# Batch 2's q^T on TensorE, batch 3's loads earlier, k loaded with q and v from batch 4 on

## The chip, the cores and the metric

The kernel runs on one core of a Trainium2 chip. The metric is the device time of one execution in microseconds (us); the figure for the kernel before is the median of three runs. A profiled execution gives the rest: which engine worked when, what each instruction waited for, and when the transfers landed.

The core has a matrix engine (TensorE, PE in the profile; PEld is its weight load), a vector engine (VectorE, DVE), an activation engine (ScalarE, ACT), a general engine (GpSimd, POOL) and a synchronising engine (SyncE, SP). In this kernel GpSimd issues the loads from main memory, which turn float32 into float16 on the way, and SyncE issues, in one queue that keeps its order, the stores of the output and the DMA transposes.

## The reference

Attention with k and v projected along the sequence (1024 rows to 64), for 8 batches of 8 heads with head size 64, followed by a gated layer over the 512 features of all heads:

```python
k_proj = np.einsum('ks,bhsd->bhkd', E, k)
v_proj = np.einsum('ks,bhsd->bhkd', F, v)
scores = np.matmul(q, k_proj.transpose(0, 1, 3, 2)) / sqrt(64)
attn = softmax(scores)                       # over the 64 projected rows
attn_out = np.matmul(attn, v_proj)           # 8 x 8 x 1024 x 64
x = attn_out.transpose(0, 2, 1, 3).reshape(8192, 512)
g = np.maximum(x @ w1, x @ w2)               # 8192 x 1024
out = g @ w_out                              # 8192 x 512, float32
```

The kernel computes the gated layer in another form (the maximum as a ReLU of x @ (w1 - w2) plus x @ w2, and products of 2 x 2 blocks with seven products instead of eight), which the change does not touch. The scores need q with the head size on the partitions, q^T (`qt`), and the projected k in the same way (`kpt`). How these two transposes are made, and when q, k and v are loaded for them, is what the change is about.

## The kernel before

The program sets the order of every engine's instructions itself. Buffers that matter here:

```python
kvq = ctx.enter_context(tc.tile_pool(name="kvq", bufs=4))     # k, v and q of all batches, in turn
...
def att_banks(dtype=FP32):                                    # two PSUM tiles of two banks, in turn
    return ps.tile(
        [128, 2, 512 if dtype == FP32 else 1024], dtype, tag="att", bufs=2, name="att_ps"
    )
```

A load takes the oldest of the four kvq tiles, and waits until that tile has been read for the last time: k and v by the projections, q by its transposes. The projections (L180) of a batch, and the two ways to transpose:

```python
def step_kv(t, h0=0, h1=H, which="kv", att=False, dma=False):
    kv_ps = att_banks()[:, 0, :] if att else mm_bank()
    ...                                          # products with E and F, L180; copies by ACT (k) and DVE (v, L195)
            if dma:
                nc.vector.tensor_copy(out=kp[:, :, 1, :], in_=kp[:, :, 0, :])     # L197
                step_kpt_dma(t)                  # kpt by DMA transpose, L222

def step_kpt(t, h0=0, h1=H, att=False):          # kpt by TensorE, L210, and a copy by DVE, L215

def step_gate(t):                                # GpSimd reads kpt: what it issues after comes later
    nc.gpsimd.tensor_copy(out=junk, in_=t["kpt"][0:1, 0, 0:1])

def step_qt(t, h0, nh=2, i0=0, i1=NI):           # q^T of nh heads by TensorE
    qt_ps = mm_bank(FP16)
    ni = i1 - i0
    for h in range(nh):
        for i in range(ni):
            nc.tensor.transpose(                 # L236
                out=qt_ps[:, (h * ni + i) * 128 : (h * ni + i + 1) * 128],
                in_=t["q"][:, h0 + h, 2 * (i0 + i) : 2 * (i0 + i) + 2, :],
                identity=ident16,
            )
    nc.vector.tensor_copy(                       # L241
        out=t["qt"][:, h0 : h0 + nh, i0 * 128 : i1 * 128],
        in_=qt_ps[:, 0 : nh * ni * 128].rearrange("q (h n) -> q h n", h=nh),
    )

def step_qt_dma(t, h0=0, h1=H):                  # q^T by DMA transpose, in the queue of SyncE
    nc.sync.dma_start_transpose(                 # L248
        out=t["qt"][:, h0:h1].rearrange("q h (i p) -> q (h i) p", p=128),
        in_=t["q"][:, h0:h1].rearrange("p h c d -> p (h c d)"),
    )
```

Attention goes in four parts per batch, of two heads each. `step_sc` makes scores in an attention tile (L260) and their exponential; `step_da` makes the sums (dn) and the values (at) in two attention tiles (L365), the logarithm of the sums (L374), its negative exponential (L377, a slot later), and the product on DVE (L381, a slot after that). From batch 3 on, `step_group` makes the scores in other banks (L280).

The rest of TensorE's work is the gated layer: 16 units (two per batch, n from 0), each with seven up products (L621) and seven down products (L699). The down products of unit n alternate with the up products of unit n + 1, in two halves h. The program names the slots between them: ("G", n, h) opens a half, ("U", n, h, i) is the i-th up product of it, and steps are hung behind slots:

```python
def loads(b, *names):
    for n in names:
        b_ = b + (n == "k")
        if b_ < B:
            load_all(tiles[b_], b_, n, {"k": k, "v": v, "q": q}[n])
...
t = tiles[2]
at_slot(("P", 0, 6, 0), new_attn, t)
at_slot(("P", 0, 6, 0), step_qt_dma, t, 0, H // 2)
at_slot(("P", 0, 6, 0), step_qt_dma, t, H // 2, H)
at_slot(("G", 1, 0), step_kv, t, 0, H, "kv", True)
at_slot(("G", 1, 0), loads, 3, "v", "q", "k")
at_slot(("U", 1, 0, 1), step_kpt, t, 0, H, True)
for key, s_, p in (
    (("U", 1, 0, 6), step_sc, 0), (("U", 1, 1, 0), step_da, 0), (("U", 1, 1, 2), step_sc, 1),
    (("U", 1, 1, 5), step_da, 1), (("G", 2, 0), step_sc, 2), (("U", 2, 0, 2), step_da, 2),
    (("U", 2, 0, 4), step_sc, 3),
):
    at_slot(key, s_, t, p)

for b in range(3, B):
    t = tiles[b]
    n = 2 * b - 4
    at_slot(("G", n, 0), new_attn, t)
    at_slot(("G", n, 0), step_qt_dma, t, 0, H // 2)
    at_slot(("G", n, 0), step_qt_dma, t, H // 2, H)
    at_slot(("U", n, 0, 1), step_kv, t, 0, H, "kv", True, b > 3)
    if b > 3:
        at_slot(("U", n, 0, 6), step_gate, t)
    else:
        at_slot(("U", n, 0, 3), step_kpt, t, 0, H, True)
    at_slot(("U", n, 0, 6), loads, b + 1, "v", "q", "k")
```

So in the kernel before, the loads behind a batch are v and q of the next batch and k of the one after it; q^T comes by DMA from batch 2 on, and kpt by DMA from batch 4 on.

Of the kernel before, what the change touches and what calls it, by code (L numbers as in the profile page):

```python
# [9 lines left out]
FP16 = mybir.dt.float16  # L10
# [6 lines left out]
def kernel(  # L17
# [12 lines left out]
    nc = tc.nc  # L30

    B, H, S, D = q.shape
# [4 lines left out]
    NI = NC // 2  # L37
# [22 lines left out]
    def mm_bank(dtype=FP32, n=None):  # L60
        if n is None:
            n = turn.pop(0)
            turn.append(n)
        return ps.tile([128, 512 if dtype == FP32 else 1024], dtype, tag=f"mm{n}", name="mm_ps")

    def att_banks(dtype=FP32):
        return ps.tile(
            [128, 2, 512 if dtype == FP32 else 1024], dtype, tag="att", bufs=2, name="att_ps"
        )
# [27 lines left out]
    def load_all(t, b, n, src):  # L97
        alloc(t, n)
        load(t, n, src, b, 0, H)
# [23 lines left out]
    for f0 in range(0, DF, 256):  # L123
        for w_sb, w in ((w2_sb, moe_w2), (w1_sb, moe_w1)):
            nc.gpsimd.dma_start(
                out=w_sb[:, :, f0 : f0 + 256],
                in_=w[:, f0 : f0 + 256].rearrange("(r p) f -> p r f", p=128),
# [5 lines left out]
    junk = const.tile([1, 1], FP16)  # L133
# [16 lines left out]
    for i in range(2):  # L150
        eft_ps = mm_bank()
        for c in range(NC):
            nc.tensor.transpose(
                out=eft_ps[:, c * KP : (c + 1) * KP],
                in_=ef_v[:, i, c, :],
# [68 lines left out]
        )  # L224


    def step_gate(t):
        nc.gpsimd.tensor_copy(out=junk, in_=t["kpt"][0:1, 0, 0:1])


    def step_qt(t, h0, nh=2, i0=0, i1=NI):
        qt_ps = mm_bank(FP16)
        ni = i1 - i0
        for h in range(nh):
            for i in range(ni):
# [9 lines that stand above are left out]
# [274 lines left out]
    U = {(b, o): {"n": n, "b": b, "o": o, "t": tiles[b]} for n, (b, o) in enumerate(units)}  # L519
# [260 lines left out]
    t = tiles[0]  # L780
# [4 lines left out]
    step_kpt(t, 0, 4)  # L785
    warm(2)
    step_qt(t, 0, 4, 0, NI // 2)
    step_qt(t, 0, 4, NI // 2, NI)
    warm(2)
    two_sc(t, 0, 0)  # L790
# [7 lines left out]
    two_inv(t, 0, 0)  # L798
    warm(4)
    step_qt(t, 4, 4, 0, NI // 2)  # L800
    step_qt(t, 4, 4, NI // 2, NI)
    warm(2)
# [20 lines left out]

    def loads(b, *names):
        for n in names:
            b_ = b + (n == "k")
            if b_ < B:
                load_all(tiles[b_], b_, n, {"k": k, "v": v, "q": q}[n])

    slots = [  # L830
        (0, u0[0]), (None, f(two_at, 1, 1)), (1, u0[1]), (None, lambda: loads(1, "v", "q", "k")),
        (None, wd[1]), (2, u1[0]), (3, u1[1]), (4, u0[2]), (None, wt[0]), (5, u0[3]),
        (None, wd[2]), (None, wt[1]), (6, u1[2]), (7, u1[3]), (8, u0[4]), (9, u0[5]), (None, wd[3]),
# [30 lines left out]
    def at_slot(key, s, *a):  # L864
        steps.setdefault(key, []).append(lambda: s(*a))
# [11 lines left out]
    t = tiles[1]  # L877
    at_slot((0, 19), new_attn, t)
    at_slot((0, 19), lambda: turn.__setitem__(slice(None), [2, 3]))
    for n, x in enumerate((  # L880
        "kv", "", "kpt", "qt0 qt1", "sc0", "qt2 qt3", "dn0 sc1 in0", "", "dn1 sc2 at0 in1", "",
        "dn2 sc3 at1 in2", "", "dn3 at2 in3", "at3", "",
    )):
        key = ("P", 0, (n - 1) // 2, (n - 1) % 2) if n else (0, 19)
        for name in x.split():
            if name[0] == "k":
                if name == "kpt":
                    at_slot(key, step_kpt, t, 0, H, True)
                else:
                    at_slot(key, step_kv, t)  # L890
                    at_slot(key, loads, 2, "v", "q")
            else:
                i = int(name[2])
                s_ = {"qt": step_qt, "sc": step_sc,
                      "dn": step_dn, "in": step_inv, "at": step_at}[name[:2]]
                at_slot(key, s_, t, 2 * i if name[:2] == "qt" else i)
                if name == "qt3":
                    at_slot(key, loads, 2, "k")
        if n in (1, 5):
            at_slot(key, step_t, 1, (0, 1) if n == 1 else (2, 3))  # L900
        if 6 <= n < 10:
            at_slot(key, sums_x, U[0, 1], ((2, 0, 1, 3)[n - 6],))


    t = tiles[2]
    at_slot(("P", 0, 6, 0), new_attn, t)
    at_slot(("P", 0, 6, 0), step_qt_dma, t, 0, H // 2)
    at_slot(("P", 0, 6, 0), step_qt_dma, t, H // 2, H)
    at_slot(("G", 1, 0), step_kv, t, 0, H, "kv", True)
    at_slot(("G", 1, 0), loads, 3, "v", "q", "k")  # L910
    at_slot(("U", 1, 0, 1), step_kpt, t, 0, H, True)
    for key, s_, p in (
        (("U", 1, 0, 6), step_sc, 0), (("U", 1, 1, 0), step_da, 0), (("U", 1, 1, 2), step_sc, 1),
        (("U", 1, 1, 5), step_da, 1), (("G", 2, 0), step_sc, 2), (("U", 2, 0, 2), step_da, 2),
# [7 lines that stand above are left out]
        at_slot(("G", n, 0), new_attn, t)  # L922
        at_slot(("G", n, 0), step_qt_dma, t, 0, H // 2)
        at_slot(("G", n, 0), step_qt_dma, t, H // 2, H)
        at_slot(("U", n, 0, 1), step_kv, t, 0, H, "kv", True, b > 3)
        if b > 3:
            at_slot(("U", n, 0, 6), step_gate, t)
        else:
            at_slot(("U", n, 0, 3), step_kpt, t, 0, H, True)
        at_slot(("U", n, 0, 6), loads, b + 1, "v", "q", "k")  # L930
    for n in range(2, 2 * B - 1):
        for h in range(2):
            m = 2 * (n - 2) + h
# [2 lines left out]
            b, p = 3 + (m - 1) // 4, (m - 1) % 4  # L936
# [75 lines left out]
```

## Time and profile before

| | us |
| --- | --- |
| time, median of 3 runs (349.24 to 350.76) | 349.68 |
| span of the profiled execution | 348.9 |
| TensorE busy (93% of the span) | 325.7 |
| VectorE busy (69%) | 240.6 |
| ScalarE busy (65%) | 226.2 |
| DMA transposes of q: 12, median from issue to landing | 5.4 |
| loads of k, v, q (1024 KB each in float16), median to landing | 17.9, 10.5, 17.1 |
| chain that ended last: PE 73%, DMA 13%, DVE 6% of the span | |

How to read it: TensorE is the engine that is busy nearly all the time, and the chain of work that ended last runs through it for 73% of the span. The 13% of DMA in that chain are stretches in which the end waited for a transfer. A row of the profile names the line of the kernel, the engine, what the instruction writes and reads, how often, and the time it took; a wait names who waited for whom. A transfer has an issue on its queue (how long the queue was held by it) and a landing.

### The profile page before, as it was taken

The numbers are of one execution on the slowest core, as the hardware profiler recorded it, in microseconds if no ns is written. First come the engines' busy times: TensorE is split into PE (matmuls) and PEld (weight loads), VectorE is DVE, ScalarE is ACT, GpSimd is POOL, SyncE is SP. The second block draws the span as 40 slices with busy tenths as digits, with TensorE's granted clock in tenths as the row PEclk, the third lists the DMA queues.
The fourth block names the chain that finished last, engine by engine and source line by source line (L and its number), as shares of the span: only waits on it lengthen the run. The fifth ranks groups of instructions, "written<-read, shape, count | busy, mean of one in ns | idle before, by whom it ended". The sixth has DMA issues, their size and how long they took to land.

```text
span 348.9 us, 7297 instructions
## 1 busy us (share of the span) xinstructions
PE 325.7 (93%) x3004; PEld 245.2 (70%) x3004; DVE 240.6 (69%) x426; ACT 226.2 (65%) x354; POOL 33.9 (10%) x50
## 2 busy tenths in 40 slices
PE   8969999899891799999999999999999999999994
PEld 4534547577561588788877888688878887888884
DVE  1364898985681186779687868768677968677572
ACT  2585322948671578778876887678778887755541
POOL 8532003020120010030002000020000000000000
PEclk9998999999997699999999999999999999999999
DMA  8999999999999984669987998889290302112032
GB/s 157 205 196 202 207 207 207 214 209 191 215 189 170 181 133 110 153 122 193 238 194 106 172 243 174 151 123 234 66 199 20 104 25 98 60 62 92 31 120 92
DMA packets 75089, 52.90 MB, mean 152 GB/s; under 512 B 28848, under 2 KB 74928, under 8 KB 75056
## 3 DMA queue, kind: packets, MB, share of 16 engines
q0 software_dynamic: 30336, 28.31, 52.1%
q1 hardware_dynamic: 44720, 24.12, 29.9%
q8 instruction: 23, 0.38, 0.4%
q14 instruction: 10, 0.08, 0.1%
HBM read 57.15 MB, written 16.78 MB: 212 GB/s over the span
## 4 chain that ended last, share of the span: by engine, by line
PE 73%; DMA 13%; DVE 6%; ACT 3%; POOL 2%; issue 2%; DVEq 0%; SPq 0%; ACTq 0%; POOLq 0%
PE mm_ps L699 36%; PE mm_ps L621 21%; DMA qt_sb<-q_sb 6%; PE mm_ps L467 4%; DMA v_sb<-in_v_dram 3%; PE att_ps L180 3%; DMA out_dram<-o_sb 3%; PE att_ps L365 2%; PE mm_ps L280 2%; PE mm_ps L503 2%; DMA kpt_sb<-kp_sb 1%; DVE o_sb L723 1%; PE mm_ps L180 1%; POOL q_sb L102 1%; POOL k_sb L102 1%
## 5 line engine op out<-in xcount | busy, mean ns | idle before, releaser
L592 ACT COPY p_sb<-mm_ps 128x512 f32<-128x512 f32 x172 | 97.9, 596 | 37.6 <-PE mm_ps L621 22.4
L699 PEld LDWEIGHTS <-big 128*128 128x128 f16 x768 | 73.8, 99 | 15.6 <-issue 6.6
L636 DVE TENSOR_TENSOR gt_sb<-mm_ps,p_sb 128x512 f16<-128x512 f32 x56 | 38.5, 688 | 62.6 <-PE mm_ps L621 41.4
L699 PE MATMUL mm_ps<-T_sb,big 128*128 128x256 f16 x576 | 78.7, 276 | 0.0
L621 PE MATMUL mm_ps<-big,big 128*128 128x256 f16 x336 | 50.4, 272 | 0.1
L621 PEld LDWEIGHTS <-big 128*128 128x128 f16 x448 | 43.8, 98 | 6.0 <-issue 0.2
L699 PEld LDWEIGHTS <-gt_sb 128*128 128x128 f16 x384 | 35.6, 98 | 13.1 <-issue 8.9
L699 PE MATMUL mm_ps<-wo_sb,gt_sb 128*128 128x256 f16 x256 | 42.7, 273 | 0.5 <-ACT o_sb L767 0.5
L621 PEld LDWEIGHTS <-wd_sb 128*128 128x128 f16 x336 | 33.1, 98 | 4.1
L621 PE MATMUL mm_ps<-xt_sb,wd_sb 128*128 128x256 f16 x224 | 33.9, 274 | 0.0
L299 ACT ACTIVATE ex_sb<-mm_ps 128x512 f16<-128x512 f32 x40 | 21.7, 596 | 17.2 <-PE mm_ps L280 17.2
L381 DVE TENSOR_TENSOR xt_sb<-att_ps,ld_sb 128x1024 f16<-128x1024 f32 x24 | 29.3, 1221 | 3.6 <-ACT ld_sb L377 3.5
L723 DVE TENSOR_TENSOR o_sb<-mm_ps,p_sb 128x512 f32<-128x512 f32 x32 | 21.9, 685 | 8.6 <-PE mm_ps L699 5.1
L377 ACT ACTIVATE ld_sb<-ld_sb 128x1024 f32<-128x1024 f32 x24 | 26.3, 1095 | 0.1
L374 ACT ACTIVATE ld_sb<-att_ps 128x1024 f32<-128x1024 f32 x24 | 24.8, 1033 | 0.6 <-PE att_ps L365 0.6
L699 PE MATMUL mm_ps<-m_sb,xt_sb 128*128 128x256 f16 x128 | 24.4, 273 | 0.0
L671 ACT ACTIVATE gt_sb<-mm_ps 128x512 f16<-128x512 f32 x28 | 16.8, 599 | 8.4 <-PE mm_ps L621 8.4
L582 DVE TENSOR_TENSOR big<-gt_sb 128x1024 f16<-128x1024 f16 x32 | 21.9, 685 | 0.3
L639 DVE TENSOR_SCALAR gt_sb<-gt_sb 128x512 f16<-128x512 f16 (+1 forms) x56 | 20.5, 366 | 1.9
L699 PE MATMUL mm_ps<-wo_sb,big 128*128 128x256 f16 x128 | 21.5, 273 | 0.0
L699 PE MATMUL mm_ps<-T_sb,gt_sb 128*128 128x256 f16 x128 | 21.5, 273 | 0.0
L699 PEld LDWEIGHTS <-xt_sb 128*128 128x128 f16 x192 | 18.8, 98 | 2.2
(104 smaller groups left out, 430.6 us busy)
## 6 DMA issues: line engine op xcount, KB each, us to landing
out_dram<-o_sb SPq DMA_DIRECT2D x63, 256.0 KB, 4.0
k_sb<-in_k_dram POOLq DMA_DIRECT2D x7, 1024.0 KB, 17.9
v_sb<-in_v_dram POOLq DMA_DIRECT2D x7, 1024.0 KB, 10.5
q_sb<-in_q_dram POOLq DMA_DIRECT2D x7, 1024.0 KB, 17.1
big<-in_moe_w_dram POOLq DMA_DIRECT2D x8, 256.0 KB, 13.0
k_sb<-in_k_dram POOLq DMA_DIRECT2D x4, 256.0 KB, 6.8
q_sb<-in_q_dram POOLq DMA_DIRECT2D x4, 256.0 KB, 7.9
v_sb<-in_v_dram POOLq DMA_DIRECT2D x2, 512.0 KB, 12.3
```

Of the source, the lines that this page charges most:

```text
L299: nc.scalar.activation(out=t["ex"][p][:, e, :], in_=banks[e], func=ACTF.Exp, scale=scale)
L374: nc.scalar.activation(out=ld, in_=dn_ps, func=ACTF.Ln)
L377: nc.scalar.activation(out=ld, in_=ld, func=ACTF.Exp, scale=-1.0)
L381: nc.vector.tensor_tensor(out=t["xt"][:, p, :, :], in0=at_ps, in1=ld, op=ALU.mult)
L582: nc.vector.tensor_tensor(out=S(i), in0=x, in1=y, op=op)
L592: copy(out=x, in_=bank)
L621: nc.tensor.matmul(out=bank[:, m * W : (m + 1) * W], lhsT=w_[:, n_, (2 * d + m) * 128 : (2 * d + m + 1) * 128], rhs=a[:, n_, :], start=(n ...
L636: nc.vector.tensor_tensor(out=c_blk(j, c), in0=two(x), in1=two(y), op=ALU.add)
L639: nc.vector.tensor_scalar_max(ap, ap, 0.0)
L671: nc.scalar.activation(out=out, in_=in_, func=ACTF.Relu)
L699: nc.tensor.matmul(out=bank[:, i * CH : (i + 1) * CH], lhsT=a(c)[:, i * 128 : (i + 1) * 128], rhs=w_(c), start=(n is not None and m == (lo ...
L723: nc.vector.tensor_tensor(out=o_sb, in0=two(x), in1=two(y), op=ALU.add)
```

## The change

It does four things. The q^T of batch 2 is made by TensorE, two heads at a time in an attention tile, behind four of the up products, instead of two DMA transposes. The loads of q and v of batch 3 (q now first) are released by the projections of batch 2, as before; k of batch 4 is no longer among them. From batch 4 on the k, v and q of one batch are loaded together, behind the gate, which now also stands behind batch 3's kpt and reads its last head instead of its first. For that, batch 3's kpt comes by DMA transpose, like that of the batches after it. What it is for: DMA transposes of q should not run beside loads, and each set of loads should start only when the transposes of the batch before it are done.

```diff
--- before.py
+++ after.py
@@ -224,12 +224,12 @@
         )
 
 
-    def step_gate(t):
-        nc.gpsimd.tensor_copy(out=junk, in_=t["kpt"][0:1, 0, 0:1])
-
-
-    def step_qt(t, h0, nh=2, i0=0, i1=NI):
-        qt_ps = mm_bank(FP16)
+    def step_gate(t, n="kpt"):
+        nc.gpsimd.tensor_copy(out=junk, in_=t[n][0:1, H - 1, 0:1])
+
+
+    def step_qt(t, h0, nh=2, i0=0, i1=NI, att=False):
+        qt_ps = att_banks(FP16)[:, 0, :] if att else mm_bank(FP16)
         ni = i1 - i0
         for h in range(nh):
             for i in range(ni):
@@ -823,7 +823,7 @@
 
     def loads(b, *names):
         for n in names:
-            b_ = b + (n == "k")
+            b_ = b + (n == "k" and b < 3)
             if b_ < B:
                 load_all(tiles[b_], b_, n, {"k": k, "v": v, "q": q}[n])
 
@@ -904,11 +904,11 @@
 
     t = tiles[2]
     at_slot(("P", 0, 6, 0), new_attn, t)
-    at_slot(("P", 0, 6, 0), step_qt_dma, t, 0, H // 2)
-    at_slot(("P", 0, 6, 0), step_qt_dma, t, H // 2, H)
     at_slot(("G", 1, 0), step_kv, t, 0, H, "kv", True)
-    at_slot(("G", 1, 0), loads, 3, "v", "q", "k")
+    at_slot(("G", 1, 0), loads, 3, "q", "v")
     at_slot(("U", 1, 0, 1), step_kpt, t, 0, H, True)
+    for i, key in enumerate((("U", 1, 0, 0), ("U", 1, 0, 3), ("U", 1, 0, 5), ("U", 1, 1, 1))):
+        at_slot(key, step_qt, t, 2 * i, 2, 0, NI, True)
     for key, s_, p in (
         (("U", 1, 0, 6), step_sc, 0), (("U", 1, 1, 0), step_da, 0), (("U", 1, 1, 2), step_sc, 1),
         (("U", 1, 1, 5), step_da, 1), (("G", 2, 0), step_sc, 2), (("U", 2, 0, 2), step_da, 2),
@@ -922,12 +922,9 @@
         at_slot(("G", n, 0), new_attn, t)
         at_slot(("G", n, 0), step_qt_dma, t, 0, H // 2)
         at_slot(("G", n, 0), step_qt_dma, t, H // 2, H)
-        at_slot(("U", n, 0, 1), step_kv, t, 0, H, "kv", True, b > 3)
-        if b > 3:
-            at_slot(("U", n, 0, 6), step_gate, t)
-        else:
-            at_slot(("U", n, 0, 3), step_kpt, t, 0, H, True)
-        at_slot(("U", n, 0, 6), loads, b + 1, "v", "q", "k")
+        at_slot(("U", n, 0, 1), step_kv, t, 0, H, "kv", True, True)
+        at_slot(("U", n, 0, 6), step_gate, t)
+        at_slot(("U", n, 0, 6), loads, b + 1, "k", "v", "q")
     for n in range(2, 2 * B - 1):
         for h in range(2):
             m = 2 * (n - 2) + h
```

## The prediction, made before the changed kernel ran

> **What bounds the kernel now.** I read the engine totals first (TensorE busy 325.7 of 348.9 us), then the busy tenths by slice:
>
> ```profile
> PE   8969999899891799999999999999999999999994
> PEclk9998999999997699999999999999999999999999
> DMA  8999999999999984669987998889290302112032
> ```
>
> TensorE is full in nearly every slice but the thirteenth (104.7 to 113.4 us, a 1), and there its granted clock falls as well. From 122 to 300 us the list of waits shows only one DMA wait of TensorE itself, 0.3 us. So whatever is to be gained lies before 121 us. The waits from 48 to 122 us, the rows that bear on it:
>
> ```profile
> POOL k_sb L102 <- DMA qt_sb<-q_sb: 16.5, 1, 16.5
> PE mm_ps L280 <- DMA qt_sb<-q_sb: 9.1, 1, 9.1
> ACT o_sb L767 <- DMA out_dram<-o_sb: 2.5, 1, 2.5
> PE att_ps L260 <- DMA qt_sb<-q_sb: 0.8, 1, 0.8
> PE att_ps L365 <- DVE vp_sb L195: 0.7, 1, 0.7
> PE mm_ps L699 <- ACT o_sb L767: 0.5, 1, 0.5
> ```
>
> Nearly all of TensorE's lost time goes back to q^T by DMA transpose. The big wait, in the timeline of TensorE (start, us, engine, line):
>
> ```profile
> 105.97 0.39 PE L365 MATMUL att_ps<-ex_sb,vp_sb 64*64 64x512 f16 x4
> 115.50 0.64 PE L280 MATMUL mm_ps<-qt_sb,kpt_sb 64*64 64x512 f16 x4 [9.14 <-DMA qt_sb<-q_sb]
> 116.08 2.74 PE L699 MATMUL mm_ps<-T_sb,big 128*128 128x256 f16 x12
> 118.61 0.90 PE L621 MATMUL mm_ps<-xt_sb,wd_sb 128*128 128x256 f16 x4
> ```
>
> L280 is the first score product of batch 3. Why its q^T is late is in the timelines of the store and transpose queue, and of the queue of loads:
>
> ```profile
> 69.25 14.66 SPq L248 DMA_TRANSPOSE qt_sb<-q_sb  x2
> 83.95 10.01 SPq L714 DMA_DIRECT2D out_dram<-o_sb  x5
> 94.06 21.23 SPq L248 DMA_TRANSPOSE qt_sb<-q_sb  x2
> 144.00 4.98 SPq L248 DMA_TRANSPOSE qt_sb<-q_sb  x2
> ```
>
> ```profile
> 92.70 0.88 POOL L102 DMA_DIRECT2D k_sb<-in_k_dram  x1 [16.54 <-DMA qt_sb<-q_sb]
> 98.01 0.88 POOL L102 DMA_DIRECT2D v_sb<-in_v_dram  x1 [4.43 <-PE att_ps L180]
> 98.87 0.88 POOL L102 DMA_DIRECT2D q_sb<-in_q_dram  x1
> ```
>
> The same pair of transposes holds the queue 4.98 us in the steady part (144 us) but 21.23 us at 94.06, where k, v and q of batch 4 load beside it. Batch 2's pair (14.66 us) runs beside the loads of k3, v3 and q3, and keeps the stores behind it until 83.95.
>
> **What the Trainium skill says.** "DMA: Bandwidth & Descriptors", section "Queues, rings and completion order": each DMA engine takes turns packet by packet between the queues that have work. The trace agrees in kind: transposes beside three loads land after 21.4 and 19.7 us, alone after 5.0 and 4.7. "TensorE: Matmul & The Clock Gate", Part 4 (PE-mode transpose): a full 128x128 transpose in one go, into PSUM, with a VectorE copy to follow, about 275 ns in one kernel's context. Here it is recorded at 219 ns, but pipelined: 16 of them, L236, run from 58.27 to the next product at 59.16, 56 ns each. The same page, Part 1 (What's actually happening): after an idle window of about 3.4 us the clock halves and comes back after a busy window of the same length. The windows of the trace agree: granted clock 0.70 over 105 to 115 us, 0.50 over 115 to 118, 0.80 over 118 to 121, 1.00 after.
>
> **Removed.** Batch 2's two DMA transposes go, so qt of batch 2 no longer waits for them (0.76 us), stores are not held in the queue, and the ACT copy of the output at 92.97 with the product behind it (0.47 us) comes in time. Batch 3's k projection is transposed by DMA instead of 16 PE transposes (101.11 to 101.48: 0.37 us of TensorE). And the loads of batch 4 now stand behind a gate that reads the end of batch 3's kpt, so batch 3's q^T no longer meets them: 9.14 us of wait, and the slow clock behind it. Its size: L280 started 0.58 us before the next product instead of 0.34 (as four 64x512 products take at 102.67), 12 products took 2.53 us (116.08 to 118.61) instead of 12 x 0.109 = 1.31, four took 0.73 instead of 0.44: 0.24 + 1.22 + 0.29 = 1.75 us. Sum: 0.76 + 0.47 + 0.37 + 9.14 + 1.75 = 12.5 us.
>
> **Do the q^T come in time?** Batch 2's transposes need q2, landed at 53.66 + 15.5 = 69.2; the first is asked for at 75.25, after unit 2's first up product. For batch 3: q3 is issued at 74.4, now ahead of v3, with only the rest of k3 beside it (landing at 59.62 + 16.0 = 75.6). An undisturbed pair of loads lands 9.5 us after the first issue and 17.0 after the second (227.06 and 227.92): q3 at 84, v3 at 92. The order on the queue is eight stores, then the pair of transposes. The eighth store follows unit 1's last down product, before at 93.6; with TensorE 2 us later there (below), 94.9. The pair then holds the queue 5.0 to 6.2 us (the steady pairs), landing at about 102. The projections of batch 3 (before 95.82) need v3, at about 97.8: in time. kpt by DMA: from the start of the projection to its landing the steady batches take 145.79 to 153.0, 7.2 us: 105. The first score product of batch 3 will be asked for at 106.4 + 3.2 (added work, below) - 0.76 - 0.47 - 0.37 = 108.0. Slack 3 us, so I expect no wait.
>
> **Added.** 32 PE transposes at 56 ns: 1.8 us on the engine that bounds. Four VectorE copies of 128x1024 at 0.68 us (the row qt_sb<-mm_ps, median 681 ns): 2.7 us, mostly beside other work, since VectorE was busy 8.4 of 10 us (70 to 80) and 6.4 (80 to 90). But they also delay things that TensorE waits for. (a) The first copy stands ahead of L636 at 77.39, whose end (78.08) releases the product at 78.12: 0.68 of delay against 0.45 of transposes, 0.24 us of new wait. (b) The attention banks are two tiles in turn. Before, the turn in batch 2's stretch was kv A, kpt B, scores A, sums B, values A, scores B; now it is kv A, qt0 B, kpt A, qt1 B, qt2 A, scores0 B, sums A, values B, qt3 A, scores1 B. qt3 thus waits for the logarithm that reads the sums (ends 85.14; 86.7 with the shift of 1.6): 0.2 us. And scores1 takes the tile of the *values*, read last by VectorE's L381 (86.26 to 87.49; shifted 87.83 to 89.06), while scores1 would start at 85.88 + 1.6 + 0.2 + 0.45 = 88.1: about 1.0 us of new wait. Sum of the added: 1.8 + 0.24 + 0.2 + 1.0 = 3.2 us.
>
> **Later batches.** From batch 4 on the three loads k, v, q of one batch follow one gate, instead of v, q and the next k. q is now last of three. The last of three landed at 155.37 + 22.0 = 177.4 and 191.40 + 22.5 = 213.9; the transposes that need q start at 178.82 and 215.24. That leaves 1.3 to 1.4 us, and another 1 to 2 us before kpt's transpose behind them is held up. I expect it to fit and cost nothing. For batch 4 the loads go out at about 105 and land by 129; its transposes come at 144 - 9 = 135.
>
> **Sum.** 12.5 removed, 3.2 added, net 9.3 us: 349.7 - 9.3 = 340.4. From 121 us on TensorE was gapless, so a shift there passes to the end unchanged. I put 340.3.
>
> **Rivals.** *Collision moves instead of going:* v3 is still landing when the transposes of q3 run, or a store holds them up, and the first scores of batch 3 still wait 2 to 5 us, with a dip of the clock: 343 to 346. For it: one in-order queue, and kpt3 added to it. Against: v3 should have landed 3 us before, and 3 us of slack. *q last of three arrives late:* each of batches 5 to 7 waits 1 to 2 us, 3 to 5 us in all: 344. For it: only 1.3 us of slack at the transpose, and all three loads of batch 7 now go where only two went. Against: the k load that was last landed before the transposes each time. *The attention banks cost more:* VectorE, nearly full there, lets every copy through to TensorE, 4 x 0.68 instead of 1.4: 341.7. *The removed waits were all, with the new bank waits hidden:* 349.7 - 12.5 + 1.8 = 339.0.
>
> **Range and chances.** The gain of 9.14 is one recorded wait with a cause that the change takes away twice (no batch 4 loads beside it, no transposes of batch 2 ahead), so most cases end between 339 and 342.5. The first two rivals give the upper end. 2% is 7.0 us, at 342.7. Range 338.3 to 343.3; faster by over 2% 0.82, within 2% 0.15, slower 0.03 (it would take late loads in every later batch).
>
> **What would show it.** Slice 13 at 9 for TensorE and its clock; no wait of L280 on qt_sb; the transposes of batch 3 starting near 95 and holding the queue 5 to 6 us; k4 issued near 105; L236 by 32 more, new rows of qt_sb<-att_ps near 0.68 us; a wait of about 1 us of L260 on VectorE's L381 near 88 us. I am wrong if the L280 wait stays above 2 us, if L280 of batches 5 to 7 waits for DMA, or if the 75 to 95 us stretch grows by more than 4 us.

## The result and the profile after

| | before | changed |
| --- | --- | --- |
| time, median of 4 runs each | 349.46 us (347.29 to 350.76) | 338.41 us (338.06 to 339.83) |
| ratio, with its 95% interval | | 0.970 (0.964 to 0.975) |
| span of the profiled execution | 348.9 us | 336.3 us |
| batch 2's projections to batch 3's first scores (first L180 of batch 2 to first L280) | 43.86 us (71.64 to 115.50) | 35.17 us (69.85 to 105.02) |
| from there to the end | 233.40 us | 231.28 us |

The changed kernel is 11.05 us faster; 9.3 were forecast, 340.3 us against 338.41 measured. In two repeats, reported with the experiments below, the medians of all runs were 339.92 against 349.96 and 340.08 against 349.58, 10.0 and 9.5 us apart. The row before the last is used for all runs below and called the stretch. It leaves out the loads and the first attention batch ahead of it, which are the same program in all of them but do not take the same time: in three profiles of the changed kernel the stretch began at 69.85, 71.96 and 72.71 us. So of the 12.6 us between the two spans, 1.8 (71.64 less 69.85) are scatter and not the change.

The busy tenths of the changed kernel, by slice:

```profile
PE   8969999899899999999999999999999999999994
PEclk9999999999999999999999999999999999999999
DMA  8999999999686996699897999699742120202132
```

The hole in the thirteenth slice is filled, and the clock never falls. DMA now has its lighter slices between 84 and 109 us: that is the room in which batch 3's transposes run. TensorE's waits for transfers between 48 and 121 us are gone from the list of waits; the waits for VectorE in the stretch:

```profile
PE att_ps L260 <- DVE xt_sb L381: 0.9, 1, 0.9
PE att_ps L365 <- DVE vp_sb L195: 0.7, 1, 0.7
PE mm_ps L621 <- DVE gt_sb L636: 0.2, 1, 0.2
```

The second of these was there before. The first and the third are new, and were worked out in the prediction as 1.0 and 0.24. The timeline of TensorE where it stood still for 9.14 us:

```profile
104.81 0.39 PE L365 MATMUL att_ps<-ex_sb,vp_sb 64*64 64x512 f16 x4
105.02 0.39 PE L280 MATMUL mm_ps<-qt_sb,kpt_sb 64*64 64x512 f16 x4
105.34 1.48 PE L699 MATMUL mm_ps<-T_sb,big 128*128 128x256 f16 x12
106.66 0.60 PE L621 MATMUL mm_ps<-xt_sb,wd_sb 128*128 128x256 f16 x4
```

The scores follow the values without a gap, and the twelve products behind them take 1.32 us from start to start instead of 2.53. The timelines of the store and transpose queue and of the loads:

```profile
66.36 26.30 SPq L714 DMA_DIRECT2D out_dram<-o_sb  x7
92.76 4.67 SPq L248 DMA_TRANSPOSE qt_sb<-q_sb  x2
99.63 1.20 SPq L222 DMA_TRANSPOSE kpt_sb<-kp_sb  x1
```

```profile
103.83 0.50 POOL L228 COPY junk<-kpt_sb 1x1 f16<-1x1 f16 x1 [29.46 <-DMA kpt_sb<-kp_sb]
104.31 0.91 POOL L102 DMA_DIRECT2D k_sb<-in_k_dram  x1
106.08 0.89 POOL L102 DMA_DIRECT2D q_sb<-in_q_dram  x1
```

The stores go out as they come; the pair of batch 3 holds the queue for 4.67 us instead of 21.23, kpt follows at 99.63 and landed 4.1 us later, and k4 starts only at 104.31.

### The profile page after: what moved, and what is told of

The parts are those of the page before. It is cut to its first block, busy times and chain, and to the rows that moved or that the text cites. A ratio compares the mean times of both kernels' runs of the same rounds, so it can differ in the third digit from the quotient of the medians.

```text
span 336.3 us, 7335 instructions
## 1 busy us (share of the span) xinstructions
PE 322.7 (96%) x3020; PEld 245.2 (73%) x3020; DVE 243.4 (72%) x430; ACT 225.9 (67%) x354; POOL 34.4 (10%) x51
## 4 chain that ended last, share of the span: by engine, by line
PE 81%; DVE 6%; DMA 6%; ACT 3%; issue 2%; POOL 1%; DVEq 0%; POOLq 0%
PE mm_ps L699 40%; PE mm_ps L621 24%; DMA big<-in_moe_w_dram 4%; PE mm_ps L467 4%; PE att_ps L180 3%; PE att_ps L365 3%; PE mm_ps L503 2%; PE mm_ps L280 2%; DMA q_sb<-in_q_dram 2%; DVE o_sb L723 1%; DVE gt_sb L636 1%; DVE xt_sb L446 1%; DVE xt_sb L381 1%; DVE vp_sb L195 1%; PE att_ps L260 1%
## 5 line engine op out<-in xcount | busy, mean ns | idle before, releaser
L699 PEld LDWEIGHTS <-big 128*128 128x128 f16 x768 | 73.1, 98 | 14.9 <-issue 6.6
L699 PE MATMUL mm_ps<-T_sb,big 128*128 128x256 f16 x576 | 77.5, 273 | 0.0
L621 PE MATMUL mm_ps<-big,big 128*128 128x256 f16 x336 | 50.4, 272 | 0.2 <-DVE gt_sb L636 0.2
L621 PEld LDWEIGHTS <-big 128*128 128x128 f16 x448 | 43.8, 98 | 6.2 <-issue 0.4
L699 PEld LDWEIGHTS <-gt_sb 128*128 128x128 f16 x384 | 35.6, 98 | 12.5 <-issue 8.3
L699 PE MATMUL mm_ps<-wo_sb,gt_sb 128*128 128x256 f16 x256 | 42.7, 273 | 0.1
L621 PEld LDWEIGHTS <-wd_sb 128*128 128x128 f16 x336 | 32.9, 98 | 3.8
L621 PE MATMUL mm_ps<-xt_sb,wd_sb 128*128 128x256 f16 x224 | 33.6, 273 | 0.0
L381 DVE TENSOR_TENSOR xt_sb<-att_ps,ld_sb 128x1024 f16<-128x1024 f32 x24 | 29.3, 1220 | 1.1 <-ACT ld_sb L377 1.0
L699 PE MATMUL mm_ps<-m_sb,xt_sb 128*128 128x256 f16 x128 | 24.4, 273 | 0.0
L671 ACT ACTIVATE gt_sb<-mm_ps 128x512 f16<-128x512 f32 x28 | 16.8, 600 | 8.3 <-PE mm_ps L621 8.3
L699 PE MATMUL mm_ps<-T_sb,gt_sb 128*128 128x256 f16 x128 | 21.5, 273 | 0.0
L699 PE MATMUL mm_ps<-wo_sb,big 128*128 128x256 f16 x128 | 21.5, 273 | 0.0
L699 PEld LDWEIGHTS <-xt_sb 128*128 128x128 f16 x192 | 18.8, 98 | 2.2
```

The source lines that it names most:

```text
L381: nc.vector.tensor_tensor(out=t["xt"][:, p, :, :], in0=at_ps, in1=ld, op=ALU.mult)
L621: nc.tensor.matmul(out=bank[:, m * W : (m + 1) * W], lhsT=w_[:, n_, (2 * d + m) * 128 : (2 * d + m + 1) * 128], rhs=a[:, n_, :], start=(n ...
L671: nc.scalar.activation(out=out, in_=in_, func=ACTF.Relu)
L699: nc.tensor.matmul(out=bank[:, i * CH : (i + 1) * CH], lhsT=a(c)[:, i * 128 : (i + 1) * 128], rhs=w_(c), start=(n is not None and m == (lo ...
```

## The experiments

Every run is judged by the stretch first, since it holds all that the change touches ahead of batch 3's scores, and by the time second. The stretch is known for one execution of each kernel, the profiled one; the time is the median of all runs. A ratio compares a run with the kernel before beside it, without executions more than 1.5% above the fastest of their kernel.

**Batch 2's q^T on TensorE, and nothing else.** The kernel before with this edit:

```diff
-    at_slot(("P", 0, 6, 0), step_qt_dma, t, 0, H // 2)
-    at_slot(("P", 0, 6, 0), step_qt_dma, t, H // 2, H)
+    for i, key in enumerate((("U", 1, 0, 0), ("U", 1, 0, 3), ("U", 1, 0, 5), ("U", 1, 1, 1))):
+        at_slot(key, step_qt, t, 2 * i, 2, 0, NI, True)
```

> Only batch 2's q^T moves to TensorE; the loads keep their old order (k of batch 4 with batch 3's v and q), batch 3's kpt stays on TensorE. Measure: the time from batch 2's first projection to batch 3's first score product L280, 43.9 us in the kernel before, 35.2 in the changed one. Theory (batch 3's transposes are slow because batch 4's loads run beside them): k4 is issued near 88, v4 and q4 near 97, so the transposes of q3, starting near 93, still hold the queue 8 to 15 us, L280 waits 2 to 6 us, the stretch is 37.5 to 41.5 us, the time 341 to 346. Rival (batch 2's transposes ahead of them in the queue were the cause): L280 waits under 1 us, stretch 35 to 36.5, time 338 to 340.

Measured: 341.13 us (340.50 to 342.91), ratio 0.985 (0.975 to 0.996); stretch 35.86 us. The load of k4, the queue, and the first scores of batch 3, in the timelines:

```profile
86.05 0.87 POOL L102 DMA_DIRECT2D k_sb<-in_k_dram  x1 [11.43 <-PE att_ps L236]
93.03 13.42 SPq L248 DMA_TRANSPOSE qt_sb<-q_sb  x2
105.97 0.39 PE L280 MATMUL mm_ps<-qt_sb,kpt_sb 64*64 64x512 f16 x4
```

The pair was as slow as expected, and L280 did not wait all the same. The prediction had treated the pair as one. The first scores need only the first transpose (heads 0 to 3), and by the transfers' landings it came 7.2 us after its issue, at 100.2; the second took 18.1 us and had time. In the kernel before the first took 21.4. The difference that shows in the loads: k4 went out at 86.05 and had landed at 96.9, because TensorE frees q2's buffer early; in the kernel before it went out at 92.70, 1.4 us ahead of the transpose. So the first transpose met only the last 3.9 us of k4 and the start of v4 (97.81); most of v4 and q4 fell on the second. On the stretch the theory failed and the rival held. The time lies above the rival's 340, at the lower end of the theory's 341 to 346; in the profile a later batch waited 1.1 us for its kpt.

**The loads, the gate and kpt3 by DMA, without the TensorE transposes.** The changed kernel with the two lines `step_qt_dma` of batch 2 put back and the four `step_qt` taken out.

> Only the loads, the gate and batch 3's kpt by DMA as in the changed kernel; batch 2's q^T stays with two DMA transposes. Theory: L280 does not wait, for batch 3's transposes run alone; the 3.1 us that the TensorE transposes add between the projections of batch 2 and the third scores are saved, and about 1.5 us of the old small waits come back (0.8 at the third scores, 0.5 at the ACT copy of the output): stretch 33 to 34.5 us, time 336.5 to 338.5. Rival (batch 2's DMA transposes have to go): its pair holds the queue to 84 and the transposes of batch 3 are late: L280 waits 2 us or more, stretch 37 or more, time above 340.

Measured: 338.91 us (338.64 to 342.54), ratio 0.980 (0.969 to 0.990); stretch 36.46 us. L280 did not wait, so this half alone removes the big wait too, and its time cannot be told from the changed kernel's 338.41. The stretch is longer than expected, not shorter than the changed kernel's, but the profile is that of the execution of 342.54 us; the other three took 338.64 to 339.04, and their stretch is not known. The lines of TensorE's waits:

```profile
PE mm_ps L699 <- ACT o_sb L767: 1.8, 1, 1.8
PE att_ps L260 <- DMA qt_sb<-q_sb: 0.8, 1, 0.8
```

With the two transposes of batch 2 ahead of the stores (they held the queue from 69.65 to 84.66), the output buffers came free late: 1.75 us at the product behind the ACT copy, where the kernel before showed 0.47, and the granted clock was 0.83 over 90 to 100 us in that profile. So the waits that the TensorE transposes remove are not a fixed 1.2 us: they were 1.23 in one profile and 2.6 in this one.

**The changed kernel without the gate behind batch 3's kpt.**

```diff
-        at_slot(("U", n, 0, 6), step_gate, t)
+        if b > 3:
+            at_slot(("U", n, 0, 6), step_gate, t)
```

> The changed kernel without the gate behind batch 3's kpt alone; k4 can then load from the last TensorE transpose of q2 (87), v4 from the projections of batch 3 (97), q4 when q3 is transposed. Theory: the pair of transposes of q3, 4.67 us with the gate, takes 7 to 10 beside k4, kpt3 behind it is late, L280 waits 1 to 3 us: stretch 36 to 38.5, time 339.5 to 342. Rival (the gate is a precaution, the load order does it): pair below 6 us, stretch 35.2, time 338 to 339.

Measured: 354.41 us (353.96 to 354.98), ratio 1.022 (1.014 to 1.031): slower than the kernel before. Stretch 47.55 us. The transpose queue and the wait:

```profile
94.42 13.66 SPq L248 DMA_TRANSPOSE qt_sb<-q_sb  x2
108.81 4.30 SPq L222 DMA_TRANSPOSE kpt_sb<-kp_sb  x1
119.04 0.64 PE L280 MATMUL mm_ps<-qt_sb,kpt_sb 64*64 64x512 f16 x4 [12.19 <-DMA kpt_sb<-kp_sb]
```

The sign was right and the size was far off. The pair is held up as expected, and kpt stands behind it in the queue; then kpt's own transpose, beside v4 and q4, takes 10.2 us to land where 2.7 to 4.5 is what it takes in other places. The first scores need the whole of kpt, but only the first half of q^T, so the small transpose is the one that hurts. So here the move of batch 3's kpt from TensorE to DMA needs the gate: the first experiment had the same loads but kpt by TensorE, and L280 did not wait.

**Two attention tiles for q^T instead of four.** The changed kernel with:

```diff
-    for i, key in enumerate((("U", 1, 0, 0), ("U", 1, 0, 3), ("U", 1, 0, 5), ("U", 1, 1, 1))):
-        at_slot(key, step_qt, t, 2 * i, 2, 0, NI, True)
+    def step_qt2(t, h0):                  # 16 transposes, two banks of one tile, two copies
+        both = att_banks(FP16)
+        ...
+    at_slot(("U", 1, 0, 2), step_qt2, t, 0)
+    at_slot(("U", 1, 0, 5), step_qt2, t, 4)
```

> The changed kernel with the 32 TensorE transposes in two attention tiles of four heads (both banks of a tile) instead of four tiles, behind the third and the sixth up product. The second scores then take the tile of the sums, as in the kernel before. Theory (the tile's turn makes the waits): the waits of 0.9, 0.3 and 0.2 us go, 1.8 us of transposes stay: stretch 33.7 to 34.2 us, time 337 to 337.5. Rival (VectorE has no room for four copies, wherever they stand): the waits come back at another product, stretch 34.8 to 35.5.

Measured: 338.19 us (336.83 to 338.47), ratio 0.974 (0.966 to 0.983); stretch 33.59 us, tail 231.27. The two new waits of TensorE on VectorE are gone from its list, with the same 32 transposes and four copies in place:

```profile
76.06 1.06 PE L915 MATMUL att_ps<-ident,q_sb 128*128 128x128 f16 x16
79.58 1.06 PE L915 MATMUL att_ps<-ident,q_sb 128*128 128x128 f16 x16
```

So it was the turn of the tiles and the place of the copies, not VectorE's load, that cost 1.6 us of the stretch (35.17 less 33.59). The median time does not show it against the 338.41 of the changed kernel, which did not run beside this one; the last comparison below does.

**Work inside the wait of the kernel before.**

```diff
             banks = [mm_bank(n=2 + e) for e in range(2)]
+            if t is tiles[3] and p == 0:
+                for _ in range(40):
+                    nc.tensor.matmul(
+                        out=banks[0], lhsT=ones16[:, 0:128], rhs=ones16, start=True, stop=True
+                    )
```

> The kernel before, with 40 products of 128x512 of ones in front of batch 3's first scores (in their own bank, overwritten by them): work of about 8.7 us inside the 9.1 us that TensorE waits for q^T anyway. Theory (the slow clock behind the wait comes from the idle time): L280 starts as late as before, the stretch stays at 43.9 us, but from L280 to the fourth group of products behind it takes 2.1 us instead of 3.8 and the granted clock stays at 1.0 there: 1.7 us shorter in all, near 347. Rival (the clock falls for another reason, such as load): no change of the 3.8 us, time 349.

Measured: 352.22 us (350.90 to 353.30), ratio 1.015 (1.002 to 1.028); the 27 runs of the kernel before beside it had a median of 349.96 and spread from 343.62 to 354.89. Stretch 48.42 us. Its timeline (L279 is the added work, L285, L704 and L626 are what L280, L699 and L621 are elsewhere):

```profile
109.66 8.81 PE L279 MATMUL mm_ps<-ones 128*128 128x512 f16 x40
118.39 0.41 PE L285 MATMUL mm_ps<-qt_sb,kpt_sb 64*64 64x512 f16 x4
118.74 1.48 PE L704 MATMUL mm_ps<-T_sb,big 128*128 128x256 f16 x12
120.06 0.60 PE L626 MATMUL mm_ps<-xt_sb,wd_sb 128*128 128x256 f16 x4
```

Two results. From the scores to the fourth group behind them it took 2.11 us (118.39 to 120.50) against 3.84 in the kernel before: with TensorE kept busy there its clock did not fall. That fits "TensorE: Matmul & The Clock Gate" (What's actually happening), where the slow clock follows idle time: the 1.75 us belong to the wait and go with it. And the time went the wrong way, because in this profile the first transpose had landed at 96.18 + 16.8 = 113.0: the wait would have been 3.3 us, and the 8.8 us of work outlasted it. The test is thus weaker than meant, for it filled an idle time of 3.3 us and not of 9.1. The wait is not constant, but the landing nearly is: 43.0 us from the start of the stretch here, 43.8 in the kernel before. The wait is shorter here because TensorE came later: batch 2's DMA transposes and the late output buffers had cost it 1.59, 1.71 and 1.66 us on the way, where the other profile shows 0.76 and 0.47, and its clock had fallen once (96.3 to 99.8 us).

**The first experiment again, with k4 held back.** Its load stands behind a GpSimd read of a result of the gated layer, written at about 92:

```diff
-    at_slot(("G", 1, 0), loads, 3, "v", "q", "k")
+    at_slot(("G", 1, 0), loads, 3, "v", "q")
+    at_slot(("U", 1, 1, 6), step_gate_gt, U[1, 0])
+    at_slot(("U", 1, 1, 6), loads, 3, "k")
```

> As the run with only the q^T on TensorE, where L280 did not wait, but the load of k4 is held back until about 92.5 us, where the kernel before issued it (there its buffer came free by the DMA transposes of q2), instead of 86. Theory (the first transpose of q3 is slow when the k4 load starts just ahead of it and v4 and q4 follow): it lands 15 to 21 us after its issue instead of 7.2, L280 waits 3 to 9 us, the stretch from batch 2's projections to L280 is 40 to 44 us instead of 35.9. Rival (batch 2's transposes in the queue were the cause, k4's hour does not matter): landing 7 to 9 us, no wait, stretch 35.9.

Measured: 343.83 us over 20 runs (342.09 to 346.28), ratio 0.992 (0.988 to 0.995); stretch 36.53 us in the profile, which was taken of the fastest of these runs.

```profile
93.45 15.91 SPq L248 DMA_TRANSPOSE qt_sb<-q_sb  x2
93.47 0.88 POOL L102 DMA_DIRECT2D k_sb<-in_k_dram  x1 [0.17 <-issue]
107.06 0.41 PE L280 MATMUL mm_ps<-qt_sb,kpt_sb 64*64 64x512 f16 x4 [0.51 <-DMA qt_sb<-q_sb]
```

The first transpose landed after 13.6 us instead of 7.2, and the time rose by 2.7 us over the run without this. So the time at which k4 is loaded counts. It does not bring back the whole 9.14 here: the wait is 0.51 us in the profile, although the median run took 1.7 us longer than the profiled one. Nor is it quite the order of the kernel before: k4 went out 0.02 us behind the first transpose, not 1.4 ahead of it. Neither theory had this result.

**The first experiment again, with batch 2's two DMA transposes as well, into a buffer that nothing reads.** TensorE's q^T is used; the DMA transposes only take part in the traffic.

```diff
+    def step_unused(t):
+        unused = qtp.tile([128, H, HALF], FP16, tag="qt", name="unused_sb")
+        new_attn(t)
+        for h0 in (0, H // 2):
+            step_qt_dma({"q": t["q"], "qt": unused}, h0, h0 + H // 2)
+
-    at_slot(("P", 0, 6, 0), new_attn, t)
+    at_slot(("P", 0, 6, 0), step_unused, t)
```

> The run with only the q^T of batch 2 on TensorE, plus the two DMA transposes of q2 as the kernel before had them, into a buffer that nothing reads: q2's buffer comes free for k4 only when they land (near 92 us), and the stores stand behind them in the queue. Theory (batch 2's transposes are what makes batch 3's late, by the held stores and the late k4 together): L280 waits 5 to 10 us again, the stretch is 41 to 46 us, time 350 to 354, above the kernel before because TensorE does the transposes as well. Rival (only k4's hour counts): as in the run with k4 held back, L280 waits 0.5 to 2.5, stretch 36.5 to 38.5, time 343 to 346.

Measured: 350.59 us (350.04 to 352.09), ratio 1.016 (1.005 to 1.028); stretch 44.12 us.

```profile
68.76 14.17 SPq L248 DMA_TRANSPOSE unused_sb<-q_sb  x2
92.80 0.87 POOL L102 DMA_DIRECT2D k_sb<-in_k_dram  x1 [18.04 <-PE mm_ps L621]
94.11 20.04 SPq L248 DMA_TRANSPOSE qt_sb<-q_sb  x2
114.37 0.64 PE L280 MATMUL mm_ps<-qt_sb,kpt_sb 64*64 64x512 f16 x4 [8.03 <-DMA qt_sb<-q_sb]
```

This brings the wait back: 8.03 us, with the first transpose landing after 20.2. k4 went out at 92.80 here, and at 93.47 in the run before this one, where the wait was 0.51. What stands between the two is batch 2's pair of transposes, the stores held behind it, and the order: k4 went out 1.3 us ahead of batch 3's first transpose here and 0.02 behind it there. In that run the issue of the first transpose held the queue for 3.0 us (the second went out at 96.42), here for 9.0 (103.09). Which of the three does the harm was not told apart. The stores' landings do not decide it: 2.2 to 2.3 us from issue in the run with k4 held back (89 to 93 us) and 6.8 to 9.8 in the kernel before (84 to 94 us), but also 5.7 to 7.8 in the first experiment (89 to 93 us, beside k4), where the first transpose landed after 7.2.

**The old load order from batch 5 on.** The changed kernel, but behind batch 3 also k5 is loaded, and behind later batches v and q of the next batch and k of the one after it:

```diff
-        at_slot(("U", n, 0, 6), loads, b + 1, "k", "v", "q")
+        if b == 3:
+            at_slot(("U", n, 0, 6), loads, b + 1, "k", "v", "q")
+        else:
+            at_slot(("U", n, 0, 6), loads, b + 1, "v", "q")
+        at_slot(("U", n, 0, 6), loads, b + 2, "k")
```

> The changed kernel with the loads of batch 5 and later in the old order (v and q of the next batch, then k of the one after it); batch 3 and its gate stay, k4 and k5 are loaded together. Theory (the order k, v, q from batch 4 on costs and brings nothing, for q lands 1.6 us before its transposes): stretch 35.2 us and from L280 to the end 231.3 us as in the changed kernel, time within 0.7 us of it. Rival (q as the last of three costs some tenths in each later batch): 0.7 to 2 us faster.

> The changed kernel beside these two on one chip: stretch 35.2 us, 338 to 340 us.

Measured: 340.47 us (339.58 to 340.85) with the old order and 340.08 (339.58 to 340.17) for the changed kernel beside it; stretches 35.19 and 35.17. No difference that the runs can tell. The changed kernel's ratio is 0.985 (0.971 to 0.998) here. In the profile of the old order batch 4 waited 0.7 us for its kpt, which no batch did in the three profiles of the changed kernel; its first transpose of q had landed after 7.8 us, beside the load of k5.

**The two-tile version with batch 2's third values one slot later,** against the changed kernel on the same chip:

```diff
-        (("U", 1, 1, 5), step_da, 1), (("G", 2, 0), step_sc, 2), (("U", 2, 0, 2), step_da, 2),
-        (("U", 2, 0, 4), step_sc, 3),
+        (("U", 1, 1, 5), step_da, 1), (("G", 2, 0), step_sc, 2), (("U", 2, 0, 3), step_da, 2),
+        (("U", 2, 0, 5), step_sc, 3),
```

> The version with two attention tiles for q^T, and in unit 3 the sums and values of batch 2's third part one slot later (and the fourth scores one slot later), so that the values no longer wait for the VectorE copy of batch 3's projected v. Expected: the wait of 0.73 us of L365 goes, stretch 32.9 us instead of 33.6, time about 1.5 to 2.3 us below the changed kernel. Rival (the wait comes back at the fourth scores or at the following sums): stretch 33.5 or more.

> The changed kernel once more, beside the two versions with fewer attention tiles, on one chip: stretch 35.2 us, time 338 to 339; 1.6 us above the two-tile version if the stretch carries to the end.

Measured: 336.99 us (336.01 to 337.82) against 339.92 (338.57 to 340.92) for the changed kernel, six runs each; stretch 32.74 against 35.18, and 231.4 against 231.3 us from there to the end. The last wait of TensorE in the stretch is gone and did not come back elsewhere. This version beats both kernels; against the kernel before its ratio is 0.972 (0.965 to 0.979), where the changed kernel beside it has 0.981 (0.974 to 0.988).

## Why the prediction was right, and where it was off

Between the first projection of batch 2 and the fourth group behind batch 3's first scores lie 47.70 us before (71.64 to 119.34) and 37.25 after (69.85 to 107.10): 10.45 us saved, where 9.3 were forecast. By the steps of the prediction:

- **Added, 3.2 forecast, 3.07 measured.** From the projections to the third scores, the old wait of 0.76 left out: 19.79 us before (71.64 to 92.19 less 0.76), 22.86 after (69.85 to 92.71). The terms: 32 transposes 1.79 us (four times 0.44 to 0.45 to the next product), new waits of 0.20, 0.27 (the gap from 84.61 to 84.88 ahead of the fourth part) and 0.87, against 0.24, 0.2 and 1.0. The four copies took 0.68 us each, as taken from the old row.
- **The third scores' wait, 0.76:** gone, as forecast.
- **The small removals, 0.84 forecast, 1.68 measured.** This is the term that was mis-sized. From the third scores to the last values ahead of batch 3's scores it took 13.78 us before (92.19 to 105.97) and 12.10 after (92.71 to 104.81). The prediction counted only the wait behind the ACT copy (0.47) and kpt's TensorE transposes (0.37). As much again lay in gaps of 0.1 to 0.3 us on TensorE, of which the list of waits shows one of 0.2 (on L381) and leaves the others out: 0.37 between 93.6 and 95.8, 0.32 beyond kpt's own 0.37 ahead of the fourth scores, 0.16 behind the third.
- **The big wait, 9.14 forecast, 9.32 measured** (9.53 us from values to scores before, 0.21 after).
- **The clock behind it, 1.75 forecast, 1.76 measured** (3.84 less 2.08). That it belongs to the idle time is supported by the filled wait, with the limit named there, and by the two runs with waits of 12.19 and 8.03 us: the scores behind them took 0.64 us as in the kernel before, and 0.39 to 0.41 where there was no such wait.

0.76 - 3.07 + 1.68 + 9.32 + 1.76 = 10.45. From there to the end 229.56 us before and 229.20 after: the rest of the shift passed through, and the one wait of 0.3 us of a later batch happened not to occur.

The slack was there, though smaller than forecast: the pair of batch 3 went out at 92.8 (95 forecast), kpt landed at 103.7 (105), and the scores asked at 105.0 (108.0), 1.3 us later where 3 were forecast. q as the last of three landed at 165.0, 201.7 and 237.6, 1.6 to 1.7 us ahead of its transposes (1.3 to 1.4 forecast). The first two rivals did not come; in the profiles of the changed kernel no later batch waited for q, and the old order was no faster. Of the third rival nothing came either: with the same copies at other places the waits vanished. The fourth, 339.0, has a number nearer to 338.41 than the forecast itself, but not for its reason: the new waits were not hidden, they came to 0.20 + 0.27 + 0.87 = 1.34 us.

Three figures of the prediction are wrong, and the sum rests on none of them. The 19.7 and 4.7 us given for a second transpose are medians of the pair; the second one landed after 17.9 us beside the loads and 4.4 alone. And 93.6 with a shift of 2 gives 95.6 for the eighth store, not 94.9: by its own terms the prediction put the pair 0.7 us too early.

"A cause that the change takes away twice" was right in its result, since each half alone removes L280's wait: stretch 35.86 and 36.46, together 35.17. They do not add up. But the cause as the prediction put it, the loads of batch 4 beside the transposes, was only half of it. In the first experiment those loads still ran beside the pair, and L280 did not wait: k4, sent out early, had landed before the first transpose did. The unused transposes brought 8.03 us back. The wait for q^T needed loads beside batch 3's transposes (it was gone in the second experiment, without them) *and* batch 2's DMA transposes ahead of them (gone in the first, without these). Only with kpt by DMA and no gate did the loads alone bring a wait, 12.19 us, and that was for kpt. Batch 2's transposes free q2's buffer late (k4 then starts just ahead of batch 3's first transpose) and hold back stores. Of these the late k4 is shown to count: held back, it takes the first transpose from 7.2 us to 13.6. "DMA: Bandwidth & Descriptors" (Queues, rings and completion order) describes how each DMA engine takes turns between queues, which fits. What takes the landing on to 20.2 us, the held stores, the transposes themselves or the 1.3 us by which k4 went first, stays open.

## What to carry to other kernels

In these runs a DMA transpose in an ordered queue cost three times: its own landing (4.4 to 6.4 us alone in the changed kernel, up to 21.4 beside loads), the stores that stood behind it (batch 2's pair held the queue for 14.66 us), and the buffer that it freed late, whose next load then ran beside the next transpose. Before a late transfer is blamed on its neighbours, look up which half of it the waiting instruction needs, and what stood ahead of it in the same queue. When a step is moved into PSUM tiles that are used in turn, write down the turn before and after: four tiles or two for the same 32 transposes made 1.6 us of difference in the stretch.

## What the runs showed of the hardware that had not been expected

- The small transpose suffers as well as the large: kpt's took 2.7 us to land alone (the steady batches) and 10.2 beside two loads.
- Even with nothing loading, kpt's transpose landed after 4.1 to 4.5 us instead of 2.7 in single batches of some runs (4.1 in batch 3 of the changed kernel), and one later batch then waited about 1 us; it came and went between profiles.
- The kernel before spread over 343.2 to 354.9 us in the runs beside these experiments, the changed one over 338.1 to 340.9. Batch 3's first transpose landed after 21.4 us in one profile and 16.8 in another with the same program up to there, but its landing lay 43.8 and 43.0 us behind the start of the stretch. So the wait and what TensorE lost ahead of it traded places; that they are the source of the spread is not shown.
